# Tokens in partitions in the second layer of a first pass, its gate factor moved into the additions, and a later phase's operands and weights prepared ahead

## The chip, the cores and the metric

One core of one Trainium2 chip runs the whole program. The metric is device time in microseconds of one execution. The matrix engine is TensorE (PE in the profile; its weight loads are PEld), the vector engine VectorE (DVE), the scalar engine ScalarE (ACT), the general one GpSimd (POOL); SP issues all DMA transfers. Matmuls accumulate in PSUM, in eight banks of 128 x 512 fp32.

## What is computed

```python
attn = ...                              # 4 x 8 heads, 576 positions, windowed and dilated
x = attn, as (2304 tokens, 512)
# first layer pair: 8 experts, every token through all of them
P = exp(x @ w_gate - max); 8 times: P /= P.sum(1); P /= P.sum(0); P *= N / E
for e in range(8):
    out += P[:, e:e + 1] * (maximum(x @ w1[e], 0.0) @ w2[e])      # 512 -> 1024 -> 512
# second layer pair
h = out @ w_in                          # 512 -> 2048
return (maximum(h, 0) ** 2) @ w_out     # 2048 -> 512
```

## The kernel before, in words

After the attention, 80 steps follow. A step takes 256 hidden columns of a layer pair: its first layer, and (in the next step) its second layer, added into `acc`. Steps 0 to 31 are the first pass over the experts with a pair of 512-token tiles and 256 "single" tokens; steps 32 to 63 the second pass, with the other pair of tiles and the same weights; steps 64 to 71 and 72 to 79 the second layer pair for the two pairs of tiles. Every fp32 operand is held as a high part (`hi`, rounded to the matmul's format) and the rest (`lo`), and a product is three matmuls.

The first layer of a pair of tiles is a 2 x 2 block product in seven products, called u1 to u7 (`l1_pair`), six matmuls each, in the banks `s` (u1, u3), `pt` (u4, u5, u6) and `xt` (u2, u7). Between them stand copies: after u1 bank `s` is copied to `pt`, after u4 and after u5 `pt` is copied out (L667, L671) before the next product goes on in it. The seven operands x are slots 0 to 6 of `x_hi` and `x_lo`, made from four blocks (`pair_pieces`, `new_operands`) with POOL subtractions, ACT casts and VectorE subtractions. The single tokens' first layer (`us`) is 24 matmuls of 256 columns. In the first pass the second layer is 8 units for the pair and 2 for the single tokens (`l2_units`), six matmuls each in one of three `mm` banks; VectorE adds each bank to `acc`. In the second pass it is seven mixed units v1 to v7 (`l2_mixed`).

In steps 3 to 31 the gate factor P is multiplied into the hidden values (`evac_g`: product on VectorE with a tile `pp` of P spread over the partitions, cast on ACT, subtraction on VectorE); before the factor is known (steps 0 to 2) `acc` is multiplied once. For the single tokens, whose second layer has tokens in partitions, P is one scalar per partition in the addition.

Weights are split in `prep_w`; the first pass stores its split weights in DRAM and the second pass fetches them. `w_in` and `w_out` come as 64-bit numbers and are narrowed on VectorE in the first pass (`narrow`, four stages a step).

The order on every engine is the order of the code: `run(u)` issues a unit and then what `after(k, f)` put k units behind it. Each engine takes its list in order; a transfer that waits holds back those behind it on SP. `xb` is a pair of 128 x 1024 load buffers that everything of that kind shares.

Of the kernel before, what the change touches and what calls it, by code (L numbers as in the profile page):

```python
# [47 lines left out]
def tile_kernel(ctx: ExitStack, tc: tile.TileContext, a):  # L48
# [34 lines left out]
    y_dram = dram.tile([128, KC, NTOK], F32, name="y_dram")  # L83
    p_dram = dram.tile([NCH, E, 128], F32, name="p_dram")
    w_dram = {
        n + h: dram.tile([NS1, 128, 1024], F32, name=f"w_{n}{h}") for n in ("blk", "sum", "w2", "mix") for h in ("h", "l")
# [56 lines left out]
    def prep_w(i):  # L143
# [16 lines left out]
        if kept(i + 1):  # L160
            w = wset[(i + 1) % 2]
            out += [(0, lambda: fetch("blk", i + 1, w["blk"])), (0, lambda: fetch("sum", i + 1, w["sum"]))]
        elif i + 1 < len(steps):
            w = wset[(i + 1) % 2]
# [9 lines left out]
            def keep(n):  # L174
                if i + 1 < NS1:
                    store(n, i + 1, w[n])

            def blk_done():
                load_w(i + 2, 0)
                keep("blk")  # L180

            out += [(0, s1), (1, s2), (2, hi(w["blk"], flat(raw1)))]
            out += [(5, lo(w["blk"], flat(raw1), blk_done))]
            out += [(10, hi(w["sum"], flat(sums))), (14, lo(w["sum"], flat(sums), lambda: keep("sum")))]
        if kept(i):
            w2 = wset[i % 2]["w2"]
            out += [(0, lambda: fetch("w2", i, w2)), (0, lambda: fetch("mix", i, mixes[i % 2]))]
            if not kept(i + 3):
                out += [(2, lambda: load_w(i + 3, 0))] if kept(i + 2) else []
            if not kept(i + 2):  # L190
                out += [(2, lambda: load_w(i + 2, 1))] if kept(i + 1) else []
# [17 lines left out]
        elif i >= 0:  # L209
            w = wset[i % 2]  # L210
            out += [(1, hi(w["w2"], raw2)), (3, lo(w["w2"], raw2, lambda: load_w(i + 1, 1)))]
# [100 lines left out]
    def load_p(pair, e, t):  # L312
        if e == E:
            pair, e = pair + 1, 0
        if pair < 2:
            p = p_t[pair, e, t] = post[0].tile([128, T], F32, tag="pp", name="pp", bufs=3)
            spread(p, e, PAIRS[pair] + t * T)
# [134 lines left out]
    def sinkhorn():  # L452
# [50 lines left out]
        for t in range(2):  # L503
            load_p(0, 0, t)
# [45 lines left out]
    def evac_g(i, ghi, glo, src, p, k):  # L550
# [12 lines left out]
        if moe and p is None:  # L563
# [3 lines left out]
        held = {"r": p}  # L567
# [11 lines left out]
        if not moe:  # L579
            after(k, square)  # L580
            k += 1
        after(k, product)
        after(k + 1, lambda: nc.scalar.copy(ghi, held["g"]))  # L583
        after(k + 2, lambda: low(held["g"], False))

    def l1_pair(i):
# [56 lines left out]
        def out(fc, t, src, k):  # L643
# [4 lines left out]
            p = p_t[pair_of(i), steps[i][1] // SPE, t] if steps[i][0] and i >= SCALED else None  # L648
            evac_g(i, gh[:, fc, cols], gl[:, fc, cols], src, p, k)
# [25 lines left out]
        def u6():  # L675
            product(bank_b, i, "blk", 3, 3, stop=True)
            out(1, 0, bank_b, 0 if i < SCALED or not steps[i][0] else 1)
# [10 lines left out]
    def l1_single(i):  # L688
        def unit(fcs):
# [16 lines left out]
            evac_g(i, gh, gl, ps, None, 0)  # L706
# [5 lines left out]
    def l2_units(i, which):  # L712
# [10 lines left out]
        by_channel = moe and not which  # L723

        def unit(c, h, w):
            ps = bank("mm")
            ps = ps[:, :w]
# [9 lines left out]
            if by_channel:  # L737
                dst = acc[which].rearrange("p (c n) -> p c n", c=KC)[:, c, h:h + w]
            else:
                dst = acc[which].rearrange("p (c d) -> p c d", d=DM)[:, c]  # L740
            ch = t0 // 128 + c
            p = ptile[:, ch, s // SPE:s // SPE + 1] if moe and which else None
# [5 lines left out]
            elif p is not None and i >= SCALED:  # L748
# [16 lines left out]
        def turn(ch, src):  # L765
# [4 lines left out]
            y = tmp("y")  # L770
# [5 lines left out]
        if by_channel:  # L776
            return [lambda c=c, h=h: unit(c, h, T) for h in range(0, n, T) for c in range(KC)]
        return [lambda c=c: unit(c, 0, DM) for c in range(n // 128)]
# [48 lines left out]
    def operands(i):  # L827

        if phase(i) == 2:
            at = (  # L830
                ((-6, -6), (1, 2, 5, 6, 6, 7, 8, 9, 9, 11, 11, 12)),
                ((11, 12), (14, 14, 15, 15, 16, 16, 17, 18, 18, 19, 20, 20)),
            )
        else:
            at = (((-6, -6), range(1, 13)), ((11, 13), range(14, 26)))
# [3 lines left out]
        return new_operands(y_dram[:, :, t0:t0 + 2 * T], at)  # L839

# [7 lines left out]
    with tc.manual_schedule():  # L848
# [153 lines left out]
        sink = sinkhorn()  # L1002
# [151 lines left out]
```

## Time and profile before

| | us |
|---|---|
| median of 3 runs | 2008.49 (2002.41 to 2009.8) |
| profiled execution | 2008.79 |
| its span, first to last instruction | 2007.0 |
| busy: TensorE, VectorE, ACT, POOL | 1947.2, 1701.5, 738.5, 616.8 |

The profile is one execution. A busy TensorE in it is one with matmuls in flight; their ends are modelled, so the times from one start to the next are the better measure. "Idle before, releaser" in a row is how long an engine stood still and what it then had waited for.

### The profile page before, as it was taken

What the parts mean: (1) busy time and instruction counts of PE and PEld (TensorE: products, weight loads), DVE (VectorE), ACT (ScalarE), POOL (GpSimd) and SP (SyncE); (2) the same over time, 40 slices, a digit from 0 to 9 for tenths busy, and PEclk for the clock granted to TensorE, in tenths of its full rate; (3) what the DMA queues carried; (4) which work ended last, traced back from release to release, by engine and by line L of the source; (5) the groups of instructions that cost most, each with busy time, mean ns of one, the idle gap of its engine ahead of it and who ended that gap; (6) DMA issues with size and microseconds to landing.
All of it is one profiled execution on the core that took longest, in us unless ns stands there. A gap on an engine that the chain in (4) does not pass through costs nothing.

```text
span 2007.0 us, 28899 instructions
## 1 busy us (share of the span) xinstructions
PE 1947.2 (97%) x11016; PEld 1607.5 (80%) x11016; DVE 1701.5 (85%) x2428; ACT 738.5 (37%) x1204; POOL 616.8 (31%) x540
## 2 busy tenths in 40 slices
PE   8989999999999999999999999999999989999999
PEld 7768788888878888887888888888888768888887
DVE  5767889998889899888778989989989998878776
ACT  3444233333233333323343333333334454445442
POOL 4532533333223333222332333323323431123120
PEclk9899999999999999999999999999999989999999
DMA  8645566566756555665675666665666432213111
GB/s 290 219 152 206 208 241 223 212 229 233 245 216 241 222 213 226 240 236 222 216 300 215 239 227 214 239 228 221 228 232 254 171 113 74 74 58 112 57 47 49
DMA packets 134331, 393.23 MB, mean 196 GB/s; under 512 B 13344, under 2 KB 38576, under 8 KB 134192
## 3 DMA queue, kind: packets, MB, share of 16 engines
q1 hardware_dynamic: 134192, 391.38, 53.2%
q8 instruction: 87, 1.43, 0.3%
q14 instruction: 52, 0.43, 0.1%
HBM read 237.11 MB, written 154.21 MB: 195 GB/s over the span
## 4 chain that ended last, share of the span: by engine, by line
PE 73%; DVE 18%; issue 4%; ACT 3%; DMA 1%; SPq 0%; POOL 0%; DVEq 0%; ACTq 0%; POOLq 0%
PE mm L735 25%; PE pt L527 14%; PE mm L795 11%; PE xt L527 8%; PE s L527 6%; PE xt L795 3%; DVE acc L749 2%; PE xt L399 2%; DVE xb L233 2%; DVE xb L247 2%; DVE xb L240 2%; DVE suml L155 2%; PE mm L701 1%; DVE xb L229 1%; DVE xb L237 1%
## 5 line engine op out<-in xcount | busy, mean ns | idle before, releaser
L753 DVE TENSOR_TENSOR acc<-mm,acc 128x512 f32<-128x512 f32 x378 | 260.0, 689 | 136.6 <-PE mm L735 129.2
L735 PE MATMUL mm<-g,w2h 128*128 128x512 f32 x1024 | 318.4, 392 | 0.0
L167 POOL TENSOR_TENSOR sums<-raw 128x256 f32<-128x256 f32 x48 | 42.8, 892 | 789.6 <-DVE suml L155 676.9
L583 ACT CAST g<-g 128x512 fp32r<-128x512 f32 x180 | 111.8, 621 | 333.7 <-DVE g L575 333.7
L735 PEld LDWEIGHTS mm<-g,w2h 128*128 128x128 f32 x1024 | 193.5, 189 | 40.6
L735 PE MATMUL mm<-g,w2l 128*128 128x512 f32 x512 | 200.2, 391 | 0.0
L809 DVE TENSOR_TENSOR acc<-mm,acc 128x512 f32<-128x512 f32 x282 | 183.7, 677 | 0.0
L629 POOL TENSOR_TENSOR r<-mix,r 128x512 f32<-128x512 f32 x32 | 42.2, 1318 | 402.4 <-DVE mix L618 370.9
L527 PE MATMUL pt<-x_hi,sumh 128*128 128x512 f32 x320 | 129.2, 404 | 31.3 <-ACT s L667 31.3
L735 PE MATMUL mm<-w2h,g 128*128 128x512 f32 x512 | 157.8, 389 | 0.4 <-DVE acc L753 0.4
L608 DVE TENSOR_TENSOR g<-r,g 128x512 fp32r<-128x512 f32 x128 | 147.1, 1150 | 12.6 <-ACT g L605 4.6
L527 PE MATMUL xt<-x_hi,sumh 128*128 128x512 f32 x320 | 125.2, 391 | 2.4 <-DVE s L672 2.4
L527 PE MATMUL xt<-x_hi,suml 128*128 128x512 f32 x320 | 125.6, 392 | 0.7
L527 PE MATMUL pt<-x_hi,suml 128*128 128x512 f32 x320 | 125.8, 393 | 0.0
L527 PE MATMUL pt<-x_lo,sumh 128*128 128x512 f32 x320 | 125.7, 393 | 0.0
L527 PE MATMUL s<-x_hi,blkh 128*128 128x512 f32 x320 | 125.7, 393 | 0.0
L527 PE MATMUL s<-x_lo,blkh 128*128 128x512 f32 x320 | 125.2, 391 | 0.0
L527 PE MATMUL s<-x_hi,blkl 128*128 128x512 f32 x320 | 125.0, 391 | 0.0
L527 PE MATMUL xt<-x_lo,sumh 128*128 128x512 f32 x320 | 124.8, 390 | 0.0
L561 DVE TENSOR_TENSOR g<-g,g 128x512 fp32r<-128x512 f32 x180 | 124.5, 699 | 0.0
L605 ACT CAST g<-mix 128x512 fp32r<-128x512 f32 x96 | 59.7, 622 | 167.3 <-DVE mix L618 102.7
L795 PE MATMUL mm<-g,mixh 128*128 128x512 f32 x384 | 119.2, 391 | 0.3 <-DVE g L608 0.3
(187 smaller groups left out, 4834.0 us busy)
## 6 DMA issues: line engine op xcount, KB each, us to landing
raw<-in_w SPq DMA_DIRECT2D x64, 512.0 KB, 5.9
w_blkh<-blkh SPq DMA_DIRECT2D x32, 512.0 KB, 6.1
w_blkl<-blkl SPq DMA_DIRECT2D x32, 512.0 KB, 6.8
w_sumh<-sumh SPq DMA_DIRECT2D x32, 512.0 KB, 4.4
w_suml<-suml SPq DMA_DIRECT2D x32, 512.0 KB, 2.7
w_w2h<-w2h SPq DMA_DIRECT2D x32, 512.0 KB, 5.5
w_w2l<-w2l SPq DMA_DIRECT2D x32, 512.0 KB, 5.9
w_mixh<-mixh SPq DMA_DIRECT2D x32, 512.0 KB, 3.9
```

Source lines behind the costliest of these rows:

```text
L155: nc.vector.tensor_tensor(out=w[1], in0=src, in1=w[0].bitcast(F32), op=ALU.subtract)
L167: tt(out=c(sums, 0), in0=c(raw1, 2), in1=c(raw1, 3), op=ALU.add)
L527: nc.tensor.matmul(ps, w[:, c], z[:, x, j], start=start and k == 0, stop=stop and k == 5, skip_group_check=True)
L561: nc.vector.tensor_tensor(out=glo, in0=z, in1=ghi.bitcast(F32), op=ALU.subtract)
L583: after(k + 1, lambda: nc.scalar.copy(ghi, held["g"]))
L605: after(k, lambda: nc.scalar.copy(b[:, 0], src))
L608: lambda: nc.vector.tensor_tensor(out=b[:, 1], in0=src, in1=b[:, 0].bitcast(F32), op=ALU.subtract),
L629: sub = lambda o, x, y: nc.gpsimd.tensor_tensor(out=o, in0=x, in1=y, op=ALU.subtract)
L735: nc.tensor.matmul(ps, lhsT, rhs, start=k == 0, stop=k == 3 * FC - 1)
L753: nc.vector.tensor_tensor(out=dst, in0=ps, in1=dst, op=ALU.add)
L795: nc.tensor.matmul(ps, w[wt][:, c], z[:, g], start=start and k == 0, stop=stop and k == 2, skip_group_check=True)
L809: nc.vector.tensor_tensor(out=o, in0=ps, in1=o, op=ALU.add)
```

## The change

In the first pass the pair's second layer takes the hidden values as stationary and the weights as moving operand, so `acc` has tokens in partitions as for the single tokens; P goes into the additions (scalar_tensor_tensor), and hidden values are relu and subtraction alone. `acc` is scaled once on ACT behind step 2's units. At the end of the pass ten chunks (before: two) are transposed on TensorE (`turn`) and stored. All second-layer units of step 31 run ahead of step 32.

For the second layer pair, four differences of blocks are made on POOL in steps 36 to 45 and kept in DRAM (`differences`); around step 63 seven finished blocks are loaded, cast and subtracted as 128 x 1024 (`made_operands`). Step 64's first-layer weights are split in step 31, where step 32's weights then have to be refetched, and fetched in step 63.

```diff
 prep_w:
+        n = i + 1
+        late = 6 if i == 2 * NS1 else 0
+        if NS1 < n <= 2 * NS1:
+            w = wset[n % 2]
+            out += [(0, lambda: fetch("blk", n, w["blk"])), (0, lambda: fetch("sum", n, w["sum"]))]
...
             def blk_done():
-                load_w(i + 2, 0)
+                if n != NS1:
+                    load_w(2 * NS1 if n + 1 == NS1 else n + 1, 0)
                 keep("blk")
...
+            at = (4, 5, 6, 8) if n == NS1 else (2, 5, 10, 14)
+            out += [(late, s1), (late + 1, s2), (late + at[0], hi(w["blk"], flat(raw1)))]
...
+            if n == NS1:
+                out += [(10, lambda: fetch("blk", n, w["blk"])), (10, lambda: fetch("sum", n, w["sum"]))]
 evac_g:
-        if moe and p is None:
+        if moe:
             after(k, lambda: nc.scalar.activation(out=ghi, in_=src, func=AF.Relu))
             after(k + 1, lambda: low(src, True))
             return
 l2_units, unit:
-                    if by_channel:
-                        lhsT, rhs = wt[:, fc, c * 128:c * 128 + 128], g[:, fc, h:h + w]
-                    else:
-                        lhsT, rhs = g[:, fc, c * 128:c * 128 + 128], wt[:, fc]
-                    nc.tensor.matmul(ps, lhsT, rhs, start=k == 0, stop=k == 3 * FC - 1)
+                    nc.tensor.matmul(
+                        ps, g[:, fc, c * 128:c * 128 + 128], wt[:, fc], start=k == 0, stop=k == 3 * FC - 1
+                    )
...
-            p = ptile[:, ch, s // SPE:s // SPE + 1] if moe and which else None
+            p = ptile[:, ch, s // SPE:s // SPE + 1] if moe else None
...
-            if i == SCALED - 1 and which:
-                nc.vector.tensor_scalar(out=dst, in0=dst, scalar1=p, scalar2=None, op0=ALU.mult)
-            elif i == SCALED - 1:
-                nc.gpsimd.tensor_tensor(out=dst, in0=dst, in1=p_t[0, 0, h // T], op=ALU.mult)
-            if last and by_channel:
-                nc.sync.dma_start(y_dram[:, c, t0 + h:t0 + h + w], dst)
-            elif last and moe:
-                after(1, lambda: turn(ch, dst))
+            if i == SCALED - 1:
+                after(1, lambda: nc.scalar.activation(out=dst, in_=dst, func=AF.Identity, scale=p))
+            if last and moe:
+                after(1, lambda: turn(ch, c, dst))
 operands:
         if phase(i) == 2:
-            at = (
-                ((-6, -6), (1, 2, 5, 6, 6, 7, 8, 9, 9, 11, 11, 12)),
-                ((11, 12), (14, 14, 15, 15, 16, 16, 17, 18, 18, 19, 20, 20)),
-            )
+            return made_operands()
+    def made_operands():
...
+            def load():
+                held.append(xb())
+                for j in range(2):
+                    nc.sync.dma_start(held[0][:, j * T:j * T + T], src[j])
...
+                lambda: nc.scalar.copy(x[0], held[0]),
+                lambda: eng.tensor_tensor(out=x[1], in0=held[0], in1=x[0].bitcast(F32), op=ALU.subtract),
...
+        for at, k, src, eng in (
+            ((-4, 1, 2), 0, y(0, 0), nc.vector),
+            ((-3, 3, 4), 4, t(0), nc.gpsimd),
+            ((2, 5, 6), 1, y(1, 0), nc.vector),
+            ((4, 7, 8), 5, t(2), nc.gpsimd),
+            ((6, 9, 10), 6, t(1), nc.vector),
+            ((8, 11, 12), 3, t(3), nc.vector),
+            ((10, 13, 14), 2, y(1, 1), nc.vector),
+        ):
+            out += zip(at, block_of(k, src, eng))
 main loop:
-                ahead, l2, l2s = l2[:-3] + l2s, l2[-3:], []
+                keep = 0 if i == NS1 else 3
+                ahead, l2, l2s = l2[:len(l2) - keep] + l2s, l2[len(l2) - keep:], []
...
+                if k == 6 and NS1 + 4 <= i < 2 * NS1 - 4:
+                    next(mixing, None)
```

ACT's list in one step of the first pass, before (`s_` are the copies of bank `pt`, L667 after u4 and L671 after u5; `g` the hidden values):

```order
L655 COPY pt<-s 128x512
L151 CAST w2h_2232<-raw_107 128x1024
L151 CAST blkh_148<-raw_105 128x1024
L583 CAST g_2237<-g 128x512
L667 COPY s_4610<-pt 128x512
L671 COPY s_4611<-pt 128x512
L583 CAST g_2237<-g 128x512 x2
```

and in such a step of the changed kernel, whose lines are other by 1 to 7:

```order
L656 COPY pt<-s 128x512
L152 CAST w2h_153<-raw_108 128x1024
L152 CAST blkh_2229<-raw_106 128x1024
L568 ACTIVATE g_2237<-s 128x512
L668 COPY s_4329<-pt 128x512
L672 COPY s_4330<-pt 128x512
L568 ACTIVATE g_2237<-s_4330 128x512
L568 ACTIVATE g_2237<-pt 128x512
```

Ahead of the copy after u4 the cast of VectorE's product is gone; relu reads bank `s` itself.

ACT's list in step 63, before, from the first operand to the copy of u5's bank and the next operands:

```order
L264 CAST x_hi<-xb 128x512
L605 CAST g_2236<-r_9177 128x512
L667 COPY s_13396<-pt 128x512
L264 CAST x_hi<-xb 128x512
L671 COPY s_13397<-pt 128x512
L264 CAST x_hi<-xb 128x512 x2
L151 CAST sumh_150<-sums 128x1024
L264 CAST x_hi<-xb 128x512 x2
```

and of the changed kernel (L857 casts the finished blocks, here of slots 1, then 5, then 6 and 3):

```order
L857 CAST x_hi<-xb 128x1024
L607 CAST g_2237<-r_9000 128x512
L668 COPY s_13221<-pt 128x512
L857 CAST x_hi<-xb 128x1024
L672 COPY s_13222<-pt 128x512
L857 CAST x_hi<-xb 128x1024 x2
L607 CAST g_2237<-mix_2240 128x512
```

The casts are fewer and twice as long, and the one of slot 5 stands ahead of the copy after u5. POOL's list there, where the four lines L631 are the mixing of a step's hidden values, of the changed kernel:

```order
L631 TENSOR_TENSOR mix_2240<-mix_2240,r_9002 128x512
L858 TENSOR_TENSOR x_lo<-xb,x_hi 128x1024 x2
L631 TENSOR_TENSOR r_9000<-mix_2240,r_9000 128x512
```

The two long subtractions of slots 4 and 5 stand between the mixing of step 62 and that of step 63; before, four weight and four operand subtractions stood there.

## Rows read from the trace of the kernel before

**Rows 1.** The page, busy time and share of the span by engine.

```profile
PE 1947.2 (97%) x11016; PEld 1607.5 (80%) x11016; DVE 1701.5 (85%) x2428; ACT 738.5 (37%) x1204; POOL 616.8 (31%) x540
```

**Rows 2.** Stretches: length, busy by engine, TensorE clock; steps 3-30, 32-62, 63-64.

```profile
194.37:958.45 764.08, 738.27 (x3529) 615.67 (x3529) 679.44 (x891) 239.26 (x336) 231.76 (x229) 1.00 0.62 228
...
994.41:1580.38 585.97, 585.62 (x2584) 484.31 (x2584) 520.54 (x754) 218.59 (x377) 189.50 (x120) 1.00 0.64 236
1580.38:1640.20 59.82, 49.36 (x193) 37.18 (x192) 58.71 (x71) 27.68 (x46) 33.78 (x26) 0.89 0.34 121
```

**Rows 3.** TensorE's waits: for whom, us in total, times, longest.

```profile
PE pt L527 <- ACT s L667: 31.3, 32, 4.7
...
PE mm L735 <- DVE acc L753: 0.4, 1, 0.4
```

**Rows 4.** Stretches as in rows 2: single steps of first pass, phase three, second pass.

```profile
315.86:342.94 27.08, 26.29 (x127) 21.91 (x127) 24.26 (x33) 8.55 (x12) 7.95 (x8) 1.00 0.65 234
1666.18:1692.16 25.98, 25.98 (x128) 21.99 (x127) 20.92 (x32) 10.26 (x16) 3.33 (x4) 1.00 0.23 72
1323.00:1342.00 19.00, 19.00 (x86) 15.73 (x85) 17.23 (x26) 6.96 (x12) 6.32 (x4) 1.00 0.59 222
```

**Rows 5.** Timelines of VectorE, ACT and TensorE: start, us, instruction, [idle before, releaser].

```profile
341.07 0.68 DVE L575 SCALAR_TENSOR_TENSOR g<-s,pp 128x512 f32<-128x512 f32 x1
...
341.78 0.62 ACT L583 CAST g<-g 128x512 fp32r<-128x512 f32 x1 [2.55 <-DVE g L575]
342.31 0.58 ACT L667 COPY s<-pt 128x512 f32<-128x512 f32 x1
...
342.94 0.50 PE L527 MATMUL pt<-x_hi,sumh 128*128 128x512 f32 x1 [0.79 <-ACT s L667]
```

**Rows 6.** Groups of instructions by form, all or in steps 3-30: busy, mean ns.

```profile
L753 DVE TENSOR_TENSOR acc<-mm,acc 128x512 f32<-128x512 f32 x226 | 155.9, 690 | 74.0 <-PE mm L735 68.3
L575 DVE SCALAR_TENSOR_TENSOR g<-s,pp 128x512 f32<-128x512 f32 x84 | 58.7, 698 | 4.2 <-PE s L527 3.2
L749 DVE SCALAR_TENSOR_TENSOR acc<-mm,ptile,acc 128x512 f32<-128x512 f32 x54 | 40.1, 742 | 0.0
...
L564 ACT ACTIVATE sg<-mm 128x512 fp32r<-128x512 f32 x29 | 17.4, 600 | 190.0 <-PE mm L701 189.8
```

**Rows 7.** The chain that ended last: start, us, what (24 short matmuls).

```profile
1663.50 2.85 PE mm L701 x24
```

**Rows 8.** Timelines of POOL in step 3 and of TensorE in step 4.

```profile
210.49 10.08 POOL L757 TENSOR_TENSOR acc<-acc,pp 128x512 f32<-128x512 f32 x6
...
232.46 0.63 PE L527 MATMUL pt<-x_lo,sumh 128*128 128x512 f32 x1
232.89 0.63 PE L527 MATMUL pt<-x_hi,suml 128*128 128x512 f32 x1
```

**Rows 9.** TensorE's timeline around the transposes of one chunk.

```profile
993.81 0.60 PE L769 MATMUL mm<-ident,acc 128*128 128x128 f32 x4
994.17 0.48 PE L527 MATMUL s<-x_hi,blkh 128*128 128x512 f32 x1
```

**Rows 10.** TensorE's timeline in step 64: first matmuls of u5 and u6.

```profile
1634.99 0.50 PE L527 MATMUL pt<-x_hi,sumh 128*128 128x512 f32 x1 [0.67 <-ACT s L667]
...
1637.33 0.50 PE L527 MATMUL pt<-x_hi,blkh 128*128 128x512 f32 x1 [0.68 <-ACT s L671]
```

**Rows 11.** Timelines of POOL and of VectorE in step 63.

```profile
1581.26 1.29 POOL L629 TENSOR_TENSOR r<-mix,r 128x512 f32<-128x512 f32 x1 [12.64 <-DVE mix L618]
...
1585.92 1.74 POOL L629 TENSOR_TENSOR mix<-mix,r 128x512 f32<-128x512 f32 x1
...
1584.73 3.48 DVE L608 TENSOR_TENSOR g<-r,g 128x512 fp32r<-128x512 f32 x2
...
1595.72 0.68 DVE L608 TENSOR_TENSOR g<-r,g 128x512 fp32r<-128x512 f32 x1
```

**Rows 12.** Transfers: KB each, median us to landing.

```profile
xb<-y_dram SPq DMA_DIRECT2D x9, 512.0 KB, 4.3
```

More of the change, by code (lines that the diff above doesn't have):

```diff
@@ L187, in prep_w @@
             out += [(0, lambda: fetch("w2", i, w2)), (0, lambda: fetch("mix", i, mixes[i % 2]))]
[L188 to L191, printed above, removed]
+            if i == 2 * NS1 - 3:
+                out += [(2, lambda: load_w(2 * NS1 + 1, 0)), (2, lambda: load_w(2 * NS1, 1))]
         elif 0 <= i < NS1:
@@ L210, in prep_w @@
             w = wset[i % 2]
-            out += [(1, hi(w["w2"], raw2)), (3, lo(w["w2"], raw2, lambda: load_w(i + 1, 1)))]
+            out += [(late + 1, hi(w["w2"], raw2)), (late + 3, lo(w["w2"], raw2, lambda: load_w(i + 1, 1)))]
         return out
@@ L502, in sinkhorn @@
             yield
-        for t in range(2):
-            load_p(0, 0, t)
     steps = (
@@ L577, in product @@
             )
[L579 to L584, printed above, removed]
+        after(k, square)
+        after(k + 1, product)
+        after(k + 2, lambda: nc.scalar.copy(ghi, held["g"]))
+        after(k + 3, lambda: low(held["g"], False))
     def l1_pair(i):
@@ L647, in out @@
             cols = slice(t * T, t * T + T)
-            p = p_t[pair_of(i), steps[i][1] // SPE, t] if steps[i][0] and i >= SCALED else None
-            evac_g(i, gh[:, fc, cols], gl[:, fc, cols], src, p, k)
+            evac_g(i, gh[:, fc, cols], gl[:, fc, cols], src, k)
         def u1():
@@ L676, in u6 @@
             product(bank_b, i, "blk", 3, 3, stop=True)
-            out(1, 0, bank_b, 0 if i < SCALED or not steps[i][0] else 1)
+            out(1, 0, bank_b, 1 if kept(i) else 0)
         def u7():
@@ L721, in l2_units, with unit @@
         t0 = SINGLE if which else PAIRS[pair_of(i)]
-        by_channel = moe and not which
-        def unit(c, h, w):
+        def unit(c):
             ps = bank("mm")
-            ps = ps[:, :w]
             k = 0
@@ L747, in unit @@
                     nc.vector.tensor_copy(dst, ps)
-            elif p is not None and i >= SCALED:
+            elif moe and i >= SCALED:
                 nc.vector.scalar_tensor_tensor(
@@ L774, in turn @@
             )
-        if by_channel:
-            return [lambda c=c, h=h: unit(c, h, T) for h in range(0, n, T) for c in range(KC)]
-        return [lambda c=c: unit(c, 0, DM) for c in range(n // 128)]
+        return [lambda c=c: unit(c) for c in range(n // 128)]
     def l2_mixed(i):
@@ L839, in operands, with differences, block_of @@
         return new_operands(y_dram[:, :, t0:t0 + 2 * T], at)
+    def differences():
+        sub = lambda o, x, y: nc.gpsimd.tensor_tensor(out=o, in0=x, in1=y, op=ALU.subtract)
+        for j in range(2):
+            b = []
+            for h in range(2):
+                z = xb()
+                nc.sync.dma_start(z, y_dram[:, 2 * h + j, :2 * T])
+                b += [z[:, :T], z[:, T:]]
+            b11, b12, b21, b22 = b
+            yield
+            for k, (o, x, y) in enumerate(((b11, b12, b11), (b12, b22, b12), (b11, b22, b11), (b21, b21, b11))):
+                sub(o, x, y)
+                nc.sync.dma_start(t_dram[k, j], o)
+                yield
+    def made_operands():
+        y = lambda h, t: [y_dram[:, 2 * h + j, t * T:t * T + T] for j in range(2)]
+        t = lambda k: [t_dram[k, j] for j in range(2)]
+        out = []
+        def block_of(k, src, eng):
+            held = []
+            def load():
+                held.append(xb())
+                for j in range(2):
+                    nc.sync.dma_start(held[0][:, j * T:j * T + T], src[j])
+            x = [z[:, k].rearrange("p j n -> p (j n)") for z in (x_hi, x_lo)]
+            return (
+                load,
+                lambda: nc.scalar.copy(x[0], held[0]),
+                lambda: eng.tensor_tensor(out=x[1], in0=held[0], in1=x[0].bitcast(F32), op=ALU.subtract),
+            )
+        for at, k, src, eng in (
[8 more added lines that the diff above has]
+            out += zip(at, block_of(k, src, eng))
+        return out
     def operands_single():
```

49 lines of the change are left out of this document (22 added, 27 removed).

## The prediction

> **What bounds the kernel now.** I read the page's engine shares first, then the stages, then TensorE's waits, then single places in order of time. TensorE is busy 97% of the span [rows 1], so at bottom only its waits and its added or removed work count. The stages [rows 2] say where it waits. The first pass in steady state (steps 3 to 30) has 738.27 us of TensorE work in 764.08; the second pass, from u1 of step 32 to the end of step 62, has no waits to speak of (585.62 of 585.97); steps 63 and 64, where the second layer pair begins, have 49.36 of 59.82 at a granted clock of 0.89. One wait is by far the largest: a product into bank `pt` waits for ACT's copy at L667, 31.3 us in 32 times [rows 3].
>
> One step of each kind shows what that costs [rows 4]. A first-pass step takes 27.08 us; a step of the second layer pair's first half, with the same list of matmuls (7 products, 8 and 2 second-layer units of six matmuls each, and 24 short ones in 2.85 us [rows 7], which leaves 1.36 for each of the 17), takes 25.98, all of it busy. So 25.98 is what the matmuls need, and each first-pass step loses 1.1.
>
> Why the copy is late stands in [rows 5], around one such wait. The fifth product u5 writes the bank that L667 copies out after u4. ACT works in program order, and ahead of the copy stands the CAST of g (L583), which needs VectorE's product with the gate tile (L575). VectorE comes to that product at 341.07, after its burst of narrowing; the CAST starts at 341.78, the copy at 342.31, u5 at 342.94. The engine late is VectorE, but it reaches TensorE only through ACT's queue.
>
> **First pass: what goes and what comes.** Removed: 116 products L575 (0.70 us each on VectorE [rows 6]), the gate-tile loads, and the CAST that waited for them. In their place ACT takes relu straight from the bank into g (0.60 us, the L564 row [rows 6], against about as much for the CAST) and VectorE subtracts as before. In the new ACT list nothing ahead of the copy after u4 waits for VectorE: copy after u1, two weight CASTs, relu of u3, copy after u4. All of these are ready by the time u4 ends, and u5 stands a whole second-layer unit (1.36 us) after u4, against a copy of 0.58 [rows 5]. So I take this wait to go to zero. VectorE's additions become scalar_tensor_tensor, 0.742 instead of 0.690 [rows 6]: 8 x 0.05 = 0.4 more per step, 4 x 0.70 = 2.8 less, from 24.26 to about 21.9 of 25.98. The comparison step has 20.92 there [rows 4] and loses nothing, although its ACT list still waits for VectorE. 28 steps of 25.98 are 727.4 against 764.08: **-36.6**. This includes the longest wait, 4.7 us in step 4 [rows 3], with the slow matmuls behind it (0.43 apart instead of 0.23, the clock at its 1.2 GHz level [rows 8]): it followed six POOL multiplications of acc in 10.08 us, and these go too. Their successors, 10 ACT scalings in step 3, stand behind VectorE's additions in ACT's queue, with 6 us of ACT time in a step where ACT has 17 idle; I price them at 0, with 2 as the upper bound if one holds the copy after u5.
>
> A rule speaks against this: the Trainium skill, "ScalarE: Activation LUTs", section "Rules for kernel authors", wants relu and multiplications on VectorE and not on ScalarE. By that rule the relu would stay with VectorE and the wait with it, a gain of 0 in these steps; the trace does not bear it out here, since ACT is busy 8.55 us of 27.08 and VectorE 24.26 [rows 4]. The same page, section "What ACT_TABLE_LOAD costs", adds 93 ns for a per-partition scale; for ten scalings an estimate of 0.9 us on ACT, hidden as the rest.
>
> The matmuls of the second layer swap stationary and moving operand. The single tokens' units already run in the new form, at the same speed (inside the 25.98). I price the swap at 0.
>
> **Border of the passes (steps 31 and 32).** Ten chunks are now turned on TensorE, two were before: eight more, each 0.36 us to the next start [rows 9]: +2.9. All second-layer units of step 31 now run ahead of step 32, so its u5 and u6 stand right behind u4 and u5 and wait for the two copies; the same sequence in step 64 waits 0.67 and 0.68 [rows 10]: +1.4. Step 32 is shorter by three units (4.1 us), so the first second-layer unit of the second pass may come before its weights: between 0 and 3, I take 1. Step 31 also prepares step 64's first-layer weights (2 CASTs, 2 subtractions, 4 POOL operations), stores them and refetches step 32's. VectorE loses four products there and gains two subtractions of twice the elements, about even; the refetch starts when its store has landed and has some 12 units until u1 of step 32. I price it at 0, upper bound 10 (rival). Together **+5.3**.
>
> **Second pass (steps 33 to 62).** Eight POOL subtractions and 12 transfers are added, one step each. POOL waits for VectorE a long time in each step (12.64 us before 1581.26, [rows 11]), so POOL has room; VectorE, 17.2 of 19.0 busy [rows 4], may be slowed by one or two operations. 0, upper bound 3.
>
> **Steps 63 and 64.** From u1 of step 63 to u1 of step 65 there are 28 units of 1.36 and one of 2.85, 40.9 us; the stage takes 59.82 [rows 2], so 18.9 are lost. VectorE is busy 58.71 of 59.82 there: its x_lo and weight subtractions push back everything else. The change takes two weight subtractions and all POOL subtractions of operands out of step 63 and makes five long x_lo on VectorE and two on POOL of fourteen short ones. What stays: u5 and u6 behind each other, 1.4. What is new is a chain through two load buffers. POOL finishes the mixes of step 62 at 1587.66, 7.3 us after u1; then x_lo of operand 4, 2 x 1.3 to 2 x 1.7 us; only then may operand 5 be loaded into its buffer (4.3 us to landing for 512 KB, [rows 12]; two halves may be quicker); ACT casts it (about 1.1, twice the elements of the 0.58 copy) and only then copies out u5's bank: 14.7 to 16.3 after u1, where u6 is due at 9 units, 12.2. That is a wait of 2.5 to 4. The same happens again for operand 3, ahead of the additions that free the banks of step 64's first unit: about 2. With VectorE's remaining lag and some matmuls at the lower clock I take 9 lost in place of 18.9: **-10**, between -17 (only the 1.4 stays) and 0.
>
> Later, step 64's weight work comes six units later and its last subtraction falls into u7: +0.5. Everything else is the same.
>
> **Sum.** 2007.0 - 36.6 + 5.3 - 10 + 0.5 = 1966.2; with the 1.8 us around the span of this execution (2008.79) **1968**. The execution stands 0.3 above the median, which I neglect.
>
> **Rivals.**
> (B) Steps 63 and 64 gain nothing. For it: POOL slows VectorE. Two subtractions beside POOL's mix take 3.48 us, one with POOL idle 0.68 [rows 11]; the change puts two long operations on POOL just there. 1968 + 10 = 1978. The Trainium skill, "GPSIMD Engine Reference", section "Specifications", says that the SBUF interface is shared and that instructions with two SBUF inputs contend; the trace agrees.
> (C) The first pass keeps half its wait, at another place: VectorE's lag meets the three `mm` banks instead of ACT's queue. Against it: 0.4 us of such waits in the whole trace before [rows 3]. 28 x 0.5 = 14: 1982.
> (D) Step 32 waits for its refetched weights: the loads of the next operands stand behind the refetch in SP's queue. About 10: 1978.
> (E) Slower: the additions, now longer, free the banks so late that every unit of the first pass waits. From 1.45 us per step on (41 us in 28 steps) it is no faster than before; for 2019 it takes 1.8. VectorE would have to need 27.8 us per step where I count 21.9.
> (F) Both borders run clean: 1958.
> (G) The change doesn't do what it says: ACT's copy still comes late for another reason, and steps 63 and 64 stay: 1968 + 36.6 = 2005.
>
> **How the numbers follow.** Chances: forecast 0.63, B 0.14, C 0.08, D 0.05, E 0.03, F 0.03, G 0.04. 0.5% is 10 us, about what a measurement of this kernel tells from no change (its three runs lie 7 us apart). Faster: all but E and G, 0.93; same: G, 0.04; slower: E, 0.03. The range takes in F's neighbourhood, B, C and D and leaves out E, G and the tails: 1955 to 1986; the likeliest case alone 1958 to 1977.
>
> **What would show it.** Right: the wait of `pt` for the copy after u4 falls from 31.3 to under 5 us; first-pass steps of 26.0; no slow matmuls at step 4; eight more transposes and two waits of 0.7 in step 32; 8 to 10 us lost in steps 63 and 64, with ACT waiting for an operand load. Wrong: a new wait in each first-pass step (for `mm` banks, or ACT for an addition), TensorE idle at u1 of step 32 behind a transfer, or steps 63 and 64 at 60 us or over.

## The result, and the profile after

The changed kernel takes 1981.86 us (median of 4 runs, 1981.16 to 1986.97), the kernel before in the same measurement 2006.3: a ratio of 0.9884, with an interval from 0.9857 to 0.9911. It is faster, by 1.2%, and the interval lies clear of 1. The forecast was 1968, with a range from 1955 to 1986 and a chance of 0.93 for faster. The way and the range were right; 24.4 us of the forecast 40 came.

The profiled execution is the longest of the four: 1986.97 with a span of 1985.2. Part of it lies where nothing that is compared here differs: u1 of step 0 starts at 117.80, in the profiles of the experiments between 112.24 and 117.63, and at 114.26 before. So stages are compared, not spans. They go from u1 of one step to u1 of another; "steps 31 to 33" is u1 of step 31 to u1 of step 34.

The engines' shares of the changed kernel, from its page:

```profile
PE 1944.2 (98%) x11048; PEld 1614.1 (81%) x11048; DVE 1635.6 (82%) x2301; ACT 747.6 (38%) x1215; POOL 610.0 (31%) x534
```

Its stages, columns as in [rows 2]: steps 3 to 30, step 7 alone, steps 31 to 33, 34 to 62, 63 and 64, 65.

```profile
198.77:926.21 727.44, 727.44 (x3531) 615.82 (x3530) 616.29 (x777) 244.47 (x346) 224.68 (x225) 1.00 0.62 233
302.69:328.67 25.98, 25.98 (x129) 21.99 (x128) 22.26 (x29) 8.49 (x12) 7.96 (x9) 1.00 0.62 236
926.21:1009.24 83.03, 76.87 (x354) 61.32 (x353) 53.71 (x70) 36.55 (x62) 23.32 (x17) 0.98 0.68 247
1009.24:1561.41 552.17, 552.17 (x2437) 457.20 (x2436) 504.74 (x725) 203.58 (x351) 193.21 (x124) 1.00 0.64 240
...
1561.41:1616.83 55.42, 47.46 (x193) 37.60 (x192) 45.98 (x58) 24.20 (x36) 22.96 (x14) 0.88 0.47 162
1616.83:1644.49 27.66, 26.63 (x127) 21.76 (x126) 22.95 (x30) 15.15 (x25) 7.35 (x8) 1.00 0.15 55
```

Of the kernel before, one stage whose row was not shown: steps 31 to 33.

```profile
958.29:1028.20 69.91, 69.56 (x322) 57.54 (x321) 51.20 (x72) 30.33 (x52) 23.64 (x16) 1.00 0.73 263
```

Steps 3 to 30 went from 764.08 [rows 2] to 727.44, 36.6 less, with TensorE busy all the time. Steps 31 to 33 went from 69.91 to 83.03, 13.1 more. Steps 63 and 64 went from 59.82 [rows 2] to 55.42, 4.4 less, and step 65 from 25.98 to 27.66. These four make 26.2 less; 2008.79 less 26.2 is 1982.6, which is the median within a microsecond. The profiled execution of the changed kernel is only 21.8 shorter; the other 4.4 lie ahead of step 3, whose u1 starts at 198.77, and at 194.21 before.

TensorE's waits, as in [rows 3]. The 31.3 us for ACT's copy are 9.7 now, and other waits have come:

```profile
PE pt L531 <- ACT s L668: 9.7, 6, 4.0
...
PE mm L729 <- DVE acc L742: 3.6, 2, 2.2
```

None of the 9.7 lies in steps 3 to 30, where before it was 25.8 in 27 times; 4.8 lie ahead of step 3 (before 3.2) and 4.9 behind step 30.

ACT in a first-pass step, to be held against [rows 5]: weight casts, relu straight from bank `s`, and the copy after u4, which waits for TensorE and for nothing else.

```profile
304.25 0.57 ACT L656 COPY pt<-s 128x512 f32<-128x512 f32 x1 [0.71 <-PE s L531]
304.74 1.06 ACT L152 CAST w2h<-raw 128x1024 fp32r<-128x1024 f32 x1
305.69 1.05 ACT L152 CAST blkh<-raw 128x1024 fp32r<-128x1024 f32 x1
306.98 0.60 ACT L568 ACTIVATE g<-s 128x512 fp32r<-128x512 f32 x1 [0.24 <-PE s L531]
308.33 0.59 ACT L668 COPY s<-pt 128x512 f32<-128x512 f32 x1 [0.76 <-PE pt L531]
```

Now the border. In step 31 VectorE, ACT and TensorE show two waits in one chain each (three timelines, one for each engine):

```profile
940.10 1.76 DVE L156 TENSOR_TENSOR suml<-sums,sumh 128x1024 fp32r<-128x1024 f32 x1
941.79 1.77 DVE L561 SCALAR_TENSOR_TENSOR g<-s,g 128x512 fp32r<-128x512 f32 x1
...
944.68 0.74 DVE L742 SCALAR_TENSOR_TENSOR acc<-mm,ptile,acc 128x512 f32<-128x512 f32 x1
...
955.33 0.69 DVE L273 TENSOR_TENSOR x_lo<-xb,x_hi 128x512 fp32r<-128x512 f32 x1 [4.22 <-ACT x_hi L270]
...
957.08 0.74 DVE L742 SCALAR_TENSOR_TENSOR acc<-mm,ptile,acc 128x512 f32<-128x512 f32 x1
```

```profile
954.68 0.62 ACT L270 CAST x_hi<-xb 128x512 fp32r<-128x512 f32 x1 [8.31 <-DMA xb<-x_dram]
```

```profile
945.47 0.72 PE L729 MATMUL mm<-w2h,g 128*128 128x512 f32 x2 [1.42 <-DVE acc L742]
...
957.88 0.74 PE L729 MATMUL mm<-w2h,g 128*128 128x512 f32 x2 [2.17 <-DVE acc L742]
```

The first: VectorE has a subtraction of step 64's weights (earlier in the step than usual) and one of hidden values ahead of an addition, and these two take 1.8 us each beside POOL; the addition that frees the bank ends at 945.4. The second: VectorE stands still for 4.22 us at a low part of an operand, because ACT waits for a load from `x_dram`; the addition behind it comes at 957.08. That load was issued right behind the refetch, and its halves landed 7.3 and 8.6 us after their issue. SP's queue:

```profile
942.31 0.37 SPq L123 DMA_DIRECT2D blkh<-w_blkh  x1
942.79 0.67 SPq L123 DMA_DIRECT2D blkl<-w_blkl  x1
943.55 0.46 SPq L123 DMA_DIRECT2D sumh<-w_sumh  x1
944.84 0.32 SPq L123 DMA_DIRECT2D suml<-w_suml  x1
945.21 0.68 SPq L316 DMA_DIRECT2D pp<-p_dram  x1
946.09 2.79 SPq L294 DMA_DIRECT2D xb<-x_dram  x2
```

In step 63, SP's queue, ACT, TensorE, and VectorE with POOL (four timelines):

```profile
1562.72 0.43 SPq L123 DMA_DIRECT2D mixl<-w_mixl  x1
1566.41 0.80 SPq L852 DMA_DIRECT2D xb<-y_dram  x2
```

```profile
1572.54 1.04 ACT L857 CAST x_hi<-xb 128x1024 fp32r<-128x1024 f32 x1 [2.64 <-DMA xb<-y_dram]
1573.49 0.61 ACT L607 CAST g<-r 128x512 fp32r<-128x512 f32 x1
1574.01 0.58 ACT L668 COPY s<-pt 128x512 f32<-128x512 f32 x1
```

```profile
1574.64 0.79 PE L531 MATMUL pt<-x_hi,sumh 128*128 128x512 f32 x1 [3.26 <-ACT s L668]
1589.43 0.74 PE L782 MATMUL mm<-g,w2h 128*128 128x512 f32 x2 [2.16 <-DVE acc L796]
1593.02 1.22 PE L782 MATMUL mm<-g,w2h 128*128 128x512 f32 x2 [1.87 <-ACT s L786]
```

```profile
1587.02 1.75 DVE L610 TENSOR_TENSOR g<-mix,g 128x512 fp32r<-128x512 f32 x1
1588.70 1.28 DVE L796 TENSOR_TENSOR acc<-mm,acc 128x512 f32<-128x512 f32 x2
...
1586.09 2.13 POOL L631 TENSOR_TENSOR r<-r,r 128x512 f32<-128x512 f32 x1
```

The copy after u4 stands behind a cast that waits for a transfer: the wait of before in another dress. The transfer is the load of slot 1. It was issued at 1566.41 and landed 5.7 us later, behind eight fetches of 512 KB issued from 1557.30 to 1562.72: step 64's first-layer weights, which come this way only since the change, and step 63's second-layer weights. The other two waits are for additions. VectorE has the subtractions of step 63's hidden values ahead of them, which take 1.75 and 1.81 us beside POOL's mixing. The granted clock of steps 63 and 64 is 0.88 on the mean, 0.89 before [rows 2]. It was 0.50 in two stretches, from 1574.64 to 1580.35 behind the wait of 3.26 and from 1593.02 to 1597.45 behind that of 1.87; there matmuls start 0.43 apart, as in [rows 8].

### The profile page after: what moved, and what is told of

The parts are those of the page before. It is cut to its first block, busy times and chain, and to the rows that moved or that the text cites. A ratio compares the mean times of both kernels' runs of the same rounds, so it can differ in the third digit from the quotient of the medians.

```text
span 1985.2 us, 28881 instructions
## 1 busy us (share of the span) xinstructions
PE 1944.2 (98%) x11048; PEld 1614.1 (81%) x11048; DVE 1635.6 (82%) x2301; ACT 747.6 (38%) x1215; POOL 610.0 (31%) x534
## 4 chain that ended last, share of the span: by engine, by line
PE 92%; DVE 4%; ACT 2%; DMA 1%; issue 1%; POOL 0%; SPq 0%; ACTq 0%; DVEq 0%; POOLq 0%
PE mm L729 31%; PE pt L531 16%; PE xt L531 10%; PE s L531 10%; PE mm L782 9%; PE mm L702 5%; PE s L782 3%; PE xt L782 3%; PE xt L405 2%; DVE suml L156 1%; PE mm L958 1%; PE s L353 1%; PE pt L390 1%; DMA xb<-x_dram 0%; DMA raw<-in_w 0%
## 5 line engine op out<-in xcount | busy, mean ns | idle before, releaser
L729 PE MATMUL mm<-w2h,g 128*128 128x512 f32 x1536 | 476.3, 391 | 3.9 <-DVE acc L742 3.6
L729 PEld LDWEIGHTS mm<-w2h,g 128*128 128x128 f32 x1536 | 288.3, 189 | 64.7 <-DVE acc L742 4.4
L742 DVE SCALAR_TENSOR_TENSOR acc<-mm,ptile,acc 128x512 f32<-128x512 f32 x290 | 216.8, 748 | 104.5 <-PE mm L729 104.2
L729 PE MATMUL mm<-w2l,g 128*128 128x512 f32 x768 | 299.8, 390 | 0.0
L729 PEld LDWEIGHTS mm<-w2l,g 128*128 128x128 f32 x768 | 144.7, 188 | 30.2
L631 POOL TENSOR_TENSOR r<-mix,r 128x512 f32<-128x512 f32 x32 | 42.2, 1319 | 402.2 <-DVE mix L620 388.6
L746 DVE TENSOR_TENSOR acc<-mm,acc 128x512 f32<-128x512 f32 x146 | 100.2, 690 | 62.8 <-PE mm L729 61.2
L568 ACT ACTIVATE sg<-mm 128x512 fp32r<-128x512 f32 (+1 forms) x35 | 19.7, 562 | 273.4 <-PE mm L702 273.4
L796 DVE TENSOR_TENSOR acc<-mm,acc 128x512 f32<-128x512 f32 x188 | 120.3, 680 | 0.6 <-PE mm L782 0.6
L702 PE MATMUL mm<-xs,blkh 128*128 128x256 f32 x640 | 115.7, 280 | 0.0
```

Of the source, the lines that this page charges most:

```text
L631: sub = lambda o, x, y: nc.gpsimd.tensor_tensor(out=o, in0=x, in1=y, op=ALU.subtract)
L702: nc.tensor.matmul(ps[:, n * NSG:n * NSG + NSG], w[:, c], z[:, kc], start=k == 0, stop=k == 3 * KC - 1)
L729: nc.tensor.matmul(ps, g[:, fc, c * 128:c * 128 + 128], wt[:, fc], start=k == 0, stop=k == 3 * FC - 1)
L742: nc.vector.scalar_tensor_tensor(out=dst, in0=ps, scalar=p, in1=dst, op0=ALU.mult, op1=ALU.add)
L746: nc.vector.tensor_tensor(out=dst, in0=ps, in1=dst, op=ALU.add)
L796: nc.vector.tensor_tensor(out=o, in0=ps, in1=o, op=ALU.add)
```

## Experiments

Experiments 1, 2 and 9 to 11 have medians of four or five executions. Experiments 3 to 8 are one execution each, and only their stages are read. Every stage comes from one profiled execution.

**1. The order of ACT's list alone.** In the kernel before, ACT's CAST of a hidden value and VectorE's subtraction behind it come one unit later; nothing else changes.

```diff
 evac_g, kernel before:
+        d = 1 if moe else 0
-        after(k + 1, lambda: nc.scalar.copy(ghi, held["g"]))
-        after(k + 2, lambda: low(held["g"], False))
+        after(k + 1 + d, lambda: nc.scalar.copy(ghi, held["g"]))
+        after(k + 2 + d, lambda: low(held["g"], False))
```

> The kernel before with one thing changed: in the first pass ACT's CAST of a hidden value and VectorE's subtraction behind it stand one unit later, so that the copy of bank pt after u4 comes ahead of the CAST. All products with the gate tile stay on VectorE. Theory (the wait is only the order of ACT's list): the wait of pt for L667 falls from 31.3 us to under 4, a first-pass step takes 26.0, u1 of step 3 to u1 of step 31 takes 727 to 733 instead of 764, the time falls by 31 to 37, to about 1972. Rival (VectorE's load is what counts, and the products had to go): with 24.3 us of VectorE work in 26 the wait moves to the mm banks, the step stays at 26.5 or over and the stage at 745 or over, the time above 1987.

Measured: 1975.28, ratio 0.985 (0.9827 to 0.9873); the interval overlaps the lower end of the changed kernel's, so this one edit does at least about as much as the whole change. Its stages (3 to 30; step 7; 31 to 33):

```profile
193.75:924.66 730.91, 728.32 (x3531) 615.65 (x3529) 668.43 (x891) 240.05 (x336) 258.20 (x229) 1.00 0.64 238
301.12:327.10 25.98, 25.98 (x129) 21.99 (x127) 23.85 (x33) 8.60 (x12) 8.94 (x9) 1.00 0.72 254
924.66:994.58 69.92, 69.57 (x323) 57.55 (x322) 51.24 (x72) 30.27 (x52) 23.12 (x16) 1.00 0.74 262
```

ACT in step 7 of this run:

```profile
306.77 0.59 ACT L668 COPY s<-pt 128x512 f32<-128x512 f32 x1 [1.59 <-PE pt L527]
307.99 0.63 ACT L584 CAST g<-g 128x512 fp32r<-128x512 f32 x1 [0.63 <-DVE g L575]
```

The CAST still waits for VectorE's product, but the copy is through before it. 33.2 of the first pass's 36.6 us come from the place of this CAST in ACT's list (and of the subtraction that follows it on VectorE), with VectorE at 23.85 of 25.98. The other 3.4 are in step 4 alone, where u6 still waits 2.07 for ACT behind VectorE's product. The border costs nothing here. The wait for the copy after u4 is 5.0 us in the whole run, none of it in steps 3 to 30; under 4 was expected. The time fell by 29, a little less than the 31 to 37 expected.

**2. The first pass alone.** The changed kernel, with `prep_w` and `operands` of before and without `differences`.

```diff
 prep_w:
-        n = i + 1
-        late = 6 if i == 2 * NS1 else 0
-        if NS1 < n <= 2 * NS1:
...
+        if kept(i + 1):
...
 operands:
-            return made_operands()
+            at = (
+                ((-6, -6), (1, 2, 5, 6, 6, 7, 8, 9, 9, 11, 11, 12)),
+                ((11, 12), (14, 14, 15, 15, 16, 16, 17, 18, 18, 19, 20, 20)),
+            )
 main loop:
-                if k == 6 and NS1 + 4 <= i < 2 * NS1 - 4:
-                    next(mixing, None)
```

> The changed kernel with the weights and operands of the second layer pair prepared as before (no early weights in step 31, no refetch, no differences kept in DRAM, fourteen short operand groups in step 63). First-pass stage 727 in both theories; steps 63 to 65 as before, 85.8. For the border, steps 31 to 33 (69.9 before, 83.0 in the changed kernel): theory, about half of the 13 us comes from the early weights and their refetch: 75 to 78 here, and a time of 1974 to 1979, faster than the changed kernel. Rival, all of it comes from the ten transposed chunks and the second-layer units run ahead: 82 to 84, and 1982 to 1986.

Measured: 1978.29, ratio 0.9866 (0.9847 to 0.9885). Steps 31 to 33 and steps 63 to 65:

```profile
919.43:996.18 76.75, 74.13 (x354) 60.43 (x353) 51.09 (x68) 34.65 (x60) 22.01 (x16) 1.00 0.68 238
...
1548.36:1635.62 87.26, 73.78 (x319) 58.95 (x318) 80.09 (x99) 41.75 (x69) 39.80 (x32) 0.94 0.29 97
```

The 13.1 us of the border divide: 6.8 belong to the transposed chunks and the units run ahead, 6.3 to the early weights. In steps 63 to 65 the preparation gains 4.2 (87.26 against 83.08). Single profiles of that stage vary: with the code of before it took 85.80 to 87.26 (expected 85.8), with the changed code 81.46 to 83.08, so the gain is 2.7 to 5.8. The second part of the change, as it is written, costs at the border about as much as it gains, or a little more; the two ratios, whose intervals overlap, do not tell the kernels apart.

**3 and 4. What the early weights cost.** First the refetch alone four units later; then also the weight operations at the places of every other step, and the refetch last.

```diff
 3:
-                out += [(10, lambda: fetch("blk", n, w["blk"])), (10, lambda: fetch("sum", n, w["sum"]))]
+                out += [(14, lambda: fetch("blk", n, w["blk"])), (14, lambda: fetch("sum", n, w["sum"]))]
 4:
-            at = (4, 5, 6, 8) if n == NS1 else (2, 5, 10, 14)
+            at = (2, 5, 10, 14)
-                out += [(10, lambda: fetch("blk", n, w["blk"])), (10, lambda: fetch("sum", n, w["sum"]))]
+                out += [(17, lambda: fetch("blk", n, w["blk"])), (17, lambda: fetch("sum", n, w["sum"]))]
```

> The changed kernel with the refetch of step 32's weights issued four units later in step 31, behind the loads of the next operands. Theory (the operand loads stand behind the refetch on SP, ACT waits for them, VectorE for ACT, and an addition behind VectorE holds an mm bank): the second wait of step 31, 2.3 us, goes, with the slow matmuls behind it, and steps 31 to 33 take 79 to 81 instead of 83.0; step 32 does not wait for its weights. Rival (the loads were late for the stores ahead of them, or the wait only moves): 82.5 to 84.

> As the run with the later refetch, with the four weight operations of step 31 also at the places that they have in every other step, and the refetch at the last place of the step. Theory: both waits of step 31 for mm banks (1.6 and 2.3 us) go, with the slow matmuls behind them: steps 31 to 33 take 76 to 78; the refetch lands well before u1 of step 32. Rival: step 32 now waits for its weights, 83 or more, or one mm wait stays, 79 to 81.

Steps 31 to 33 of the two (one row each):

```profile
922.77:1001.81 79.04, 74.89 (x354) 60.28 (x353) 54.17 (x70) 36.47 (x62) 22.57 (x17) 1.00 0.73 259
```

```profile
920.40:999.08 78.68, 74.42 (x354) 60.50 (x353) 52.31 (x70) 36.17 (x62) 23.45 (x17) 1.00 0.74 260
```

With the later refetch the operand loads landed after 4.4 us (median). The wait of 2.17 us is gone, and the 4.0 us gained fit the theory (the mean clock of the stage goes from 0.98 to 1.00 as well). The usual places take away the wait of 1.42 too, yet the stage gains only 0.4 more and misses the expected 76 to 78: a new wait of 1.60 comes. ACT, then TensorE, in the fourth run:

```profile
959.83 0.58 ACT L760 COPY raw<-mm 128x512 f32<-128x512 f32 x1 [3.48 <-DMA y_dram<-raw]
```

```profile
960.46 0.73 PE L729 MATMUL mm<-w2h,g 128*128 128x512 f32 x2 [1.60 <-ACT raw L760]
```

The refetch now runs beside the stores of the transposed chunks. The fifth copy of a chunk needs the buffer of the first, whose store landed 9.0 us after its issue (2.4 in the changed kernel). Moved later, the same four transfers hit the next user of the queues.

**5. Three units kept back.**

```diff
-                keep = 0 if i == NS1 else 3
+                keep = 3
```

> The changed kernel with the last three second-layer units of step 31 kept back and put between the products of step 32, as the kernel before has it. Theory (u5 and u6 of step 32 wait 0.84 and 0.85 us, with slow first matmuls, because no unit stands between them and the copies): both waits go, steps 31 to 33 take 81.1 instead of 83.0. Rival (the chunks turned among the products, or a late addition, cost as much): 82.5 to 84.

Steps 31 to 33:

```profile
919.84:1000.11 80.27, 75.70 (x355) 61.26 (x354) 53.09 (x70) 36.01 (x62) 23.36 (x17) 0.98 0.74 255
```

Both waits are gone. The stage takes 2.8 less than 83.03, against 1.9 expected. Runs with the changed kernel's code there gave 82.51 and 83.79, so the surplus is within what this stage varies.

**6. Relu on VectorE.**

```diff
-            after(k, lambda: nc.scalar.activation(out=ghi, in_=src, func=AF.Relu))
+            after(k, lambda: nc.vector.tensor_scalar(out=ghi, in0=src, scalar1=0.0, scalar2=None, op0=ALU.max))
```

> The changed kernel with the relu of the first pass on VectorE instead of ACT: about 2.5 us more for VectorE in each step, 24.4 of 25.98. Theory (what counted was that a CAST waiting for VectorE stood ahead of ACT's copy): ACT's list still has nothing that waits for VectorE's burst ahead of the copy after u4, a step stays at 26.0 and u1 of step 3 to u1 of step 31 at 727 to 731. As the prediction put the rule on relu and VectorE: the wait stays with it, 27.1 per step and 764. Rival between them: VectorE's list is now so full that the additions hold the mm banks, 735 to 750.

Steps 3 to 30, step 7, steps 31 to 33:

```profile
197.70:925.14 727.44, 727.44 (x3531) 615.82 (x3529) 666.60 (x917) 162.58 (x206) 234.82 (x225) 1.00 0.62 233
301.62:327.60 25.98, 25.98 (x129) 21.99 (x127) 24.00 (x34) 5.55 (x7) 8.57 (x8) 1.00 0.61 231
925.14:1011.60 86.46, 77.57 (x354) 61.91 (x353) 56.52 (x76) 33.40 (x56) 22.70 (x17) 0.96 0.65 236
```

The first pass doesn't notice on which engine relu runs. At the border the second wait is 4.01, against 2.17 to 2.94 in three runs with relu on ACT. VectorE is not short of time there: it stands still for 6.07 us until ACT casts an operand, whose load landed 9.2 to 9.8 us after its issue (7.3 to 8.6 in the changed kernel). Whether the relu's place made the load later is not shown.

**7 and 8. Step 63.** First the casts one unit later, behind the copies of `pt`; then (in the changed kernel) the two low parts of POOL on VectorE.

```diff
 7:
-            ((2, 5, 6), 1, y(1, 0), nc.vector),
-            ((4, 7, 8), 5, t(2), nc.gpsimd),
-            ((6, 9, 10), 6, t(1), nc.vector),
-            ((8, 11, 12), 3, t(3), nc.vector),
-            ((10, 13, 14), 2, y(1, 1), nc.vector),
+            ((2, 6, 7), 1, y(1, 0), nc.vector),
+            ((4, 8, 9), 5, t(2), nc.gpsimd),
+            ((7, 10, 11), 6, t(1), nc.vector),
+            ((9, 12, 13), 3, t(3), nc.vector),
+            ((11, 14, 15), 2, y(1, 1), nc.vector),
 8:
-            ((-3, 3, 4), 4, t(0), nc.gpsimd),
+            ((-3, 3, 4), 4, t(0), nc.vector),
-            ((4, 7, 8), 5, t(2), nc.gpsimd),
+            ((4, 7, 8), 5, t(2), nc.vector),
```

> The changed kernel with the casts and subtractions of the finished blocks of slots 1, 5, 6, 3 and 2 one unit later in step 63, so that ACT has the copies of bank pt after u4 and u5 ahead of the casts that wait for a transfer. Theory (u5's wait of 3.4 us is ACT's copy behind a cast whose transfer is late, and the slow matmuls after it follow from it): steps 63 to 65 take 76 to 79 instead of 83.1. Rival (the stage is bound by VectorE's list, and the wait moves to the additions): 81 to 84.

> The changed kernel with the low parts of slots 4 and 5 on VectorE instead of POOL. Theory of contention (two operations of 2.4 and 2.8 us on POOL slow VectorE's, 3.5 us for two subtractions that take 1.3 alone): VectorE gets two operations of 1.2 us more and is relieved of as much or more, steps 63 to 65 take 79 to 82 instead of 83.1. Rival (VectorE's list is what the stage waits for, and POOL's own mixing is what it collides with): 84 to 88.

Steps 63 to 65, and 63 and 64 alone, of the seventh; then of the eighth:

```profile
1556.23:1635.19 78.96, 70.69 (x320) 56.71 (x318) 68.79 (x88) 39.31 (x60) 30.88 (x22) 0.98 0.38 133
1556.23:1607.52 51.29, 44.02 (x194) 34.95 (x192) 45.83 (x58) 24.16 (x36) 23.52 (x14) 0.97 0.49 174
```

```profile
1559.54:1641.71 82.17, 73.09 (x319) 58.42 (x318) 70.48 (x90) 39.30 (x60) 25.13 (x20) 0.94 0.37 128
```

The total of the seventh, 78.96, is the expected one, but only in part for the expected reason. u5's wait falls from 3.26 to 1.49, and another, for ACT's copy behind the additions, grows from 1.87 to 3.01: TensorE's idle time in steps 63 and 64 is 7.27 against 7.96. Most of the rest is the clock, 0.97 against 0.88: of the two stretches at 0.50 the one behind u5's wait is gone, and 3.1 us at 0.52 are left, behind the wait of 3.01. In runs nine and ten the same order gave 81.48 and 81.00 at a clock of 0.96; the runs whose code there is unchanged lie between 81.46 and 83.08. So what the reordering gains is between nothing and 4 us, and the rival, a wait that moves, holds for the idle time. In the eighth 82.17 lies among the unchanged ones: no difference is seen between POOL and VectorE making these two low parts.

**9 to 11. Put together.** Nine is the changed kernel with edits 4, 5 and 7. Ten is experiment 1 (the second layer of the first pass as before) with `differences`, `made_operands` and `prep_w` of experiments 4 and 7. Eleven is ten with the last three blocks loaded and made later, into step 64:

```diff
-            ((7, 10, 11), 6, t(1), nc.vector),
-            ((9, 12, 13), 3, t(3), nc.vector),
-            ((11, 14, 15), 2, y(1, 1), nc.vector),
+            ((9, 15, 18), 6, t(1), nc.vector),
+            ((10, 18, 20), 3, t(3), nc.vector),
+            ((19, 22, 24), 2, y(1, 1), nc.vector),
```

> The changed kernel with three of the edits tried singly: the usual places for step 31's weights with the refetch last, three units of step 31 kept back for step 32, and the casts behind the copies in step 63. Theory (the three losses are independent): steps 31 to 33 at 76 to 77.5 (83.0 in the changed kernel), steps 63 to 65 at 78.5 to 79.5 (83.1), first-pass stage 727.4, the time about 1972. Rival (the edits share what they gain): 79 and 81, about 1977.

> The kernel before with its CAST one unit later (second layer of the first pass as it was, products on VectorE), plus the early operands and weights of the second layer pair in their better places (weights at the usual places in step 31, refetch last, casts behind the copies). Theory (the border costs what the ten turned chunks and the hurried weights cost, and neither is here): steps 3 to 30 at 731, 31 to 33 at 70 to 72, 63 to 65 at 78.5 to 80.5, the time 1967 to 1971: faster than the changed kernel by about 12. Rival (the early weights cost 4 to 6 at the border wherever they are put): 74 to 76 there and 1972 to 1976.

> As the run before it with the last three finished blocks (slots 6, 3 and 2) loaded, cast and subtracted 2 to 10 units later, within step 64, where VectorE has gaps. Theory (the rest lost in step 63 is additions behind the long subtractions on VectorE): steps 63 to 65 at 73.5 to 76.5, the time 2 to 5 below the run before it. Rival (VectorE is merely as full in step 64, or ACT's copies of the mixed banks and not the additions are late): 78 or over, and the same time.

| | us | ratio to before | steps 3-30 | 31-33 | 63-65 |
|---|---|---|---|---|---|
| before | 2006.99 | | 764.08 | 69.91 | 85.80 |
| nine | 1972.54 | 0.9826 (0.9809 to 0.9842) | 727.43 | 77.15 | 81.48 |
| ten | 1970.01 | 0.9814 (0.9799 to 0.9829) | 730.88 | 70.76 | 81.00 |
| eleven | 1966.82 | 0.9797 (0.9782 to 0.9812) | 731.68 | 70.71 | 77.01 |

Steps 31 to 33 of ten, and steps 63 to 65 of eleven:

```profile
922.92:993.68 70.76, 70.18 (x323) 57.39 (x322) 53.64 (x74) 32.08 (x54) 23.83 (x18) 1.00 0.78 290
```

```profile
1549.95:1626.96 77.01, 70.92 (x319) 56.80 (x318) 68.08 (x88) 39.17 (x60) 28.97 (x22) 0.98 0.38 136
```

Where only the two chunks of before are turned, the early weights cost 0.8 us at the border (70.76 against 69.92 in experiment 1). In ten the last wait of step 63 was 4.17, for ACT's copy behind VectorE's additions, and those stood behind a low part of 2.36 us and a subtraction of hidden values of 1.74, both beside POOL's mixing; in eleven it is 1.97. In steps 63 to 65 none of the three met its range: nine and ten lie above theirs, and eleven, with 77.01, lies between its theory and its rival. The ratios of all three lie below the changed kernel's 0.9884 by 0.6% to 0.9%, their intervals below its own. Those of ten and eleven overlap; what tells them apart is one profile of the stage each, where TensorE's idle time in steps 63 and 64 falls from 8.27 to 5.08.

## Why the prediction was right, and where it was off

**First pass.** Forecast -36.6, measured -36.6: steps of 25.98, no slow matmuls at step 4, nothing for the swap of operands or for the longer additions. The cause named, ACT's order, is shown by experiment 1. One sentence of this part was wrong: that relu on VectorE would leave the wait with it. Experiment 6 ran so, with relu straight into `g` and no CAST on ACT, and took 727.44. What held ACT was not the engine of the relu but a CAST that needed VectorE ahead of the copy. The rule of the Trainium skill ("ScalarE: Activation LUTs", section "Rules for kernel authors") wants relu on VectorE; here the time of the 28 steps is the same with either engine, 727.44. One sign was set too low: the wait for the copy after u4 fell to 9.7 and not to under 5, since the 31.3 also held waits outside these steps, and one of 3.26 came in step 63.

**Border.** Forecast +5.3, measured +13.1; this is half of the miss. The parts that were priced came near their prices: in experiment 2, where only they remain, the border costs 6.8 against 5.3, and u5 and u6 of step 32 wait 0.68 each, as forecast. The failed step is the sentence that prices step 31's weights and the refetch at 0. It looked at u1 of step 32, which indeed did not wait, and at VectorE's sum of work, which was nearly even (53.71 us in steps 31 to 33 against 51.20). It did not follow who stands behind the refetch on SP: the operand loads, then ACT's cast, VectorE's low part, an addition, an `mm` bank. It cost 6.3, inside the bound of 10. Rival D named the queue, but put the wait in step 32.

**Steps 63 to 65.** Forecast -10 + 0.5, measured -4.4 + 1.7; in the terms of experiment 2, -4.2 in all. The mechanism of the first wait was right: an operand's cast ahead of ACT's copy, waiting for a load. Its place was one link off: not slot 5's load behind POOL, ahead of u6, but slot 1's behind the fetches of weights, ahead of u5. Its size was right (3.26, forecast 2.5 to 4), though this is partly luck, since it is another load; the forecast's own terms give 15.3 to 16.1 and not 14.7 to 16.3. The second, "the same" for operand 3, was wrong in its cause: the additions were late without a wait of VectorE for that operand, behind subtractions of hidden values that took 1.75 and 1.81 us beside POOL's mixing. Mis-sized was the total loss, taken as 9 over the 40.9 us of matmuls: 55.42 is 14.5 over. Of these 7.96 are idle time, where the forecast's waits add up to 5.9 to 7.4. The other 6.6 are matmuls that took longer, most of them in the two stretches at a granted clock of 0.50, and for these and VectorE's lag the forecast had left only 1.6 to 3.1. In step 65 two waits (0.54 and 0.49) came where one term of 0.5 was forecast. Rival B (no gain here) came nearer than the forecast in size; the two operations that it blamed, low parts on POOL, are not seen to be its cause (experiment 8), but the contention that it named is in the rows, with POOL's mixing.

**Sum.** 7.8 of the border and 6.8 of steps 63 to 65 make 14.6; the median is 13.9 above the forecast. The sum of rival G leaves out a term: with steps 63 and 64 as before as well, 1968 + 36.6 + 10 is 2015 and not 2005. The clock of steps 63 and 64, between 0.88 and 0.97, is worth about 3 us and follows the stretches behind the long waits. Behind u5's wait of 3.26 there is one, behind the 1.5 that is left of it in runs seven, nine and ten there is none. Behind the wait for ACT's copy, 3.01 in seven and 4.15 and 4.17 in nine and ten, the clock was 0.52 for 3.1 us in seven, and on the mean 0.64 and 0.68 in the 8.5 and 8.0 us that followed in nine and ten. What sets how long it stays low is open.

## What to carry to other kernels

When an engine that is far from full makes the busiest one wait, look first at what stands ahead in its list: here, moving a CAST (and the subtraction that follows it) behind the copy gave nine tenths of what a rewrite of the layer gave in the first pass, and none of its cost at the border. A transfer put in to make something early has to be followed through the queue to those behind it, and from there to the banks, and not only to its own user. Where a stage has several waits, count idle time and clock apart before saying which edit helped.

## What was not expected of the hardware

The same subtraction of 128 x 1024 on VectorE took 1.21 us in step 63 of run ten while POOL stood idle, and 2.36 while POOL was mixing hidden values; one of 128 x 512 took 0.69 and, beside the mixing, 1.74. In the changed kernel five such long ones end a fixed time after the POOL instruction beside them. For 128 x 512 this is 0.55 us (943.56 after 943.01 in step 31; 1588.77 after 1588.22 and 1591.71 after 1591.16 in step 63), for 128 x 1024 it is 1.08 (941.86 after 940.78, 1587.10 after 1586.02). Alone they take 0.68 and 1.21. By these rows VectorE's instruction does not run slower but stands still until POOL's is through; no run here tests this by itself.

A store of a transposed chunk landed after 2.4 us in the changed kernel, and after 9.0 in experiment 4, where four 512 KB fetches had been issued just ahead of it.
